# Moving one v chunk and the v tail ahead of the next batch's k and q halves, with a head pair's transposes exchanged to match

## The chip, the cores and the metric

One core of a Trainium2 chip runs the whole program. Times are device microseconds (us); the lower the better. A timed figure is the median of several executions. A profile is of one execution, with a trace of every engine. The span of an execution, from its first instruction to its last, is about 1.8 us shorter than its timed figure, so timed figures are compared with timed figures and spans with spans. A run counts as slow when it takes over 1.5% more than the fastest of the same kernel. The record also has the mean clock granted to TensorE in nearly every timed execution. Ratios are the mean time of one kernel's fast runs over the mean of the other's fast runs in the same rounds, so they are not quite the ratio of the medians that are quoted.

## The reference

Causal attention by blocks of 64 (8 batches, 8 heads, 576 positions, head size 64) is followed by a feed-forward layer with a gate, over 4608 tokens.

```
scores = (q @ k^T) / sqrt(64);  masked where block(i) < block(j), blocks of 64
attn   = softmax(scores) @ v                      # per batch and head
x      = attn as [4608, 512]
xn     = x / sqrt(mean(x*x) + 1e-6) * rms_g
out    = (silu(xn @ w_gate) * (xn @ w_val)) @ w_out
```

## The kernel before

The kernel is one long list of steps in a fixed order. Each engine executes its share strictly in that order, so a step that has to wait holds up everything behind it on its engine. Two strings matter here. INIT is the order of the first loads on GpSimd's queue, RAMP the order of the first compute steps.

```python
INIT = """
k1 q2 id k2 q1 k3 q3 v0 v1 v3 Ka Qa Kb Qb v2 vt W1 W0 W3 W2 qt O0 O1 VT V0 V2 V1 V3 h1 h0 h2 h7
h4 h3 h6 h5
"""
RAMP = """
... n0 Z n1 nr D11 D10 Z nx t3 Z a0 p D22 Z D12 D23 Z D20 a1 D21 D31 t0 D32 a2 D33 D30
nt t1 a3 t2 A0 U l l U U l U m0 U U m2 U B1 ...        # cut
"""
```

- `v0` to `v3`, `vt`: batch 0's v in four chunks of 128 positions, and its tail of 64 (two small transfers). `Ka Kb Qa Qb`: batch 1's k and q in halves of four heads. `W0` to `W3`: the gate and value weights in four blocks, two transfers each. `O0 O1`: the output weights WO in halves. `V..`: batch 1's v. `qt`, `h..`: tails and heads for batch 2.
- `t0` to `t3`: transposes on TensorE of batch 1's head pairs; t0 needs Ka and Qa, t3 needs Kb and Qb. They are first used much later, at `A0`.
- `a0`: the values of batch 0's first "late" head pair (query tiles 2 to 4). It needs every v chunk and the tail.
- `Dxy`: scores and exponentials of the late pairs. `nx`: a scaling on VectorE and ScalarE. `Z`: a dummy matmul that keeps TensorE's clock up. `U`: up projections of the feed-forward layer. `O`: one third of a down projection, four matmuls with WO. The other letters stay in their order and don't matter here.

```python
def values(self, part):                              # a0: every v chunk is read
    ...
    for j, t in enumerate(self.qts):
        for c in range(t + 1):
            mm(X[:, o:o + D + 1], self.PT[:, c0:c0 + P],
               VN[self.b % 2][:, c, 2 * self.hp + h, 0:D + 1], c == 0, c == t)

def load_down_weights(m0, m1):                       # O0: 0 to 6, O1: 6 to 12
    pool_dma(out=WO[:, m0:m1, :], in_=...)

def down(i, s, part):                                # O: four of twelve matmuls
    for m in range(part * 4, part * 4 + 4):
        mm(po, HT[:, m, s * P:(s + 1) * P], WO[:, m, :], m == 0, m == NMC - 1)
```

So the first down projection needs O1 at its seventh matmul. Transfers issued by GpSimd share eight semaphores in turn. In the order of instructions each of them waits, before it is issued, for the landing of the one eight places ahead.

The softmax here doesn't subtract the row's maximum and nothing guards it: scores larger than these inputs give would overflow.

## Time and profile before

| | before |
|---|---|
| timed, median (first runs; then with the runs beside the changed kernel) | 379.09; 379.18 us |
| span of the profiled run | 377.1 us |
| TensorE busy | 363.1 us (96%) |
| TensorE idle for the k and the q half at t3 | 1.30 + 1.08 us |
| granted clock from 20.15 to 24.40 us | 0.60 |
| first up projection | 32.23 us |
| first WO matmul | 45.35 us |

TensorE is nearly always busy, so a gain has to come from the few waits at the beginning. The rows are shown in the prediction. In a timeline row the first number is the start, the second the time, and a bracket at the end tells how long the engine had been idle and for whom.

### The profile page before, as it was taken

The page shows a single profiled execution, that of the slowest core. Times are in us where ns is not written, and L with a number is a line of the kernel's source. Part 1 is how long each engine was busy: PE and PEld are TensorE (multiplying, and loading weights), DVE is VectorE, ACT ScalarE, POOL GpSimd, SP SyncE. Part 2 cuts the span into 40 slices and gives each one's busy share as a digit, 9 for nine tenths or more (in the row PEclk, how much of TensorE's full clock was granted, in tenths as well). Part 3 has the DMA queues.
Part 4 walks back from the last instruction along what each step waited for, and adds up shares of the span by engine and source line. Part 5 has one row for each costly group of instructions (what it writes and reads, how often), then busy time and mean ns, then how long its engine had stood idle before and what let it go on. Part 6 is the DMA issues. An engine that isn't in the chain of part 4 may idle for free.

```text
span 377.1 us, 7796 instructions
## 1 busy us (share of the span) xinstructions
PE 363.1 (96%) x2953; PEld 188.3 (50%) x2993; DVE 248.9 (66%) x635; ACT 212.8 (56%) x368; POOL 138.7 (37%) x193
## 2 busy tenths in 40 slices
PE   8789999989999999999999999999999999999996
PEld 3458668645455445544454435544554444444442
DVE  6646867878875697648954894569668806724750
ACT  3967767865667657656683668267754313313321
POOL 8653697894887819446805000000000000000000
PEclk9989999999999999999999999999999999999999
DMA  9999999999999999998999427042101320011002
GB/s 161 183 202 200 183 142 158 154 168 142 167 133 185 181 92 137 178 138 84 133 152 95 95 49 141 30 98 42 51 30 28 92 83 29 2 55 56 2 20 92
DMA packets 158519, 41.12 MB, mean 109 GB/s; under 512 B 145169, under 2 KB 153873, under 8 KB 158482
## 3 DMA queue, kind: packets, MB, share of 16 engines
q0 software_dynamic: 103488, 18.59, 67.4%
q1 hardware_dynamic: 54258, 21.74, 28.9%
q8 instruction: 23, 0.38, 0.4%
q10 hardware_dynamic: 736, 0.30, 0.4%
q14 instruction: 14, 0.11, 0.1%
HBM read 37.75 MB, written 9.44 MB: 125 GB/s over the span
## 4 chain that ended last, share of the span: by engine, by line
PE 68%; DVE 14%; DMA 7%; issue 5%; ACT 3%; POOL 2%; DVEq 0%; ACTq 0%; POOLq 0%
PE f L122 63%; PE s L122 4%; DVE HT L116 4%; DVE th L116 3%; DVE XS L116 3%; DMA QKT<-QKN 3%; DMA HT<-in_q_dram 3%; POOL HT L102 1%; DMA XT<-XS 1%; ACT PT L116 1%; DVE XN L116 1%; DVE a L116 1%; ACT th L116 1%; ACT sq L116 1%; POOL VN L102 1%
## 5 line engine op out<-in xcount | busy, mean ns | idle before, releaser
L122 PE MATMUL f<-XT,WG 128*128 128x512 bf16 (+1 forms) x461 | 109.5, 357 | 2.2 <-DVE HT L116 0.6
L122 PE MATMUL f<-XT,WV 128*128 128x512 bf16 (+1 forms) x474 | 110.0, 357 | 1.0 <-DVE HT L116 0.6
L116 ACT ACTIVATE th<-f 128x512 f32<-128x512 f32 x108 | 64.6, 598 | 78.9 <-PE f L122 77.6
L116 ACT ACTIVATE PT<-s 128x1024 bf16<-128x1024 f32 (+2 forms) x100 | 95.6, 992 | 22.4 <-PE s L122 18.7
L116 DVE SCALAR_TENSOR_TENSOR th<-th,f 128x512 f32<-128x512 f32 x108 | 73.9, 684 | 48.1 <-ACT th L116 47.5
L122 PE MATMUL f<-WO,HT 128*128 128x512 bf16 x419 | 99.1, 379 | 1.0
L116 DVE TENSOR_TENSOR HT<-th,f 128x512 bf16<-128x512 f32 x108 | 74.1, 686 | 14.0 <-PE f L122 5.7
L122 PEld LDWEIGHTS <-WV 128*128 128x128 bf16 x480 | 46.8, 98 | 47.3 <-issue 1.3
L122 PEld LDWEIGHTS <-WG 128*128 128x128 bf16 x480 | 45.7, 98 | 45.4 <-issue 3.1
L122 PEld LDWEIGHTS <-HT 128*128 128x128 bf16 x432 | 40.7, 98 | 47.4 <-DVE HT L116 3.0
L102 POOL DMA_DIRECT2D QKN<-in_k_dram x60 | 47.0, 784 | 24.4 <-DMA QKT<-QKN 8.7
L102 POOL DMA_DIRECT2D QKN<-in_q_dram x60 | 47.0, 783 | 13.0 <-DMA VN<-in_v_dram 4.3
L116 ACT ACTIVATE ob<-f 128x512 f32<-128x512 f32 x36 | 21.5, 598 | 48.0 <-PE f L122 48.0
L102 POOL DMA_DIRECT2D VN<-in_v_dram x48 | 38.5, 861 | 19.6 <-PE f L122 17.1
L122 PE MATMUL f<-VN,PT 128*128 128x65 bf16 x960 | 37.8, 194 | 1.5 <-DVE XN L116 0.4
L122 PEld LDWEIGHTS <-PT 128*128 128x128 bf16 x960 | 34.5, 98 | 9.0 <-issue 2.2
L116 DVE TENSOR_TENSOR XN<-f,rd 128x320 f32<-128x320 f32 (+2 forms) x64 | 31.5, 491 | 2.2
L116 DVE MEMSET PT<- 64x64 uint32 (+1 forms) x116 | 11.4, 114 | 27.5 <-ACT PT L116 25.3
L116 DVE SCALAR_TENSOR_TENSOR XS<-XN,y,grow 128x512 bf16<-128x512 f32 x38 | 27.5, 748 | 0.4
L116 ACT ACTIVATE sq<-XN 128x512 bf16<-128x512 f32 x38 | 23.8, 627 | 2.0 <-DVE XN L116 1.7
L122 PE MATMUL s<-QKT 64*128 64x512 bf16 (+4 forms) x240 | 21.9, 294 | 0.0
L116 DVE RECIPROCAL rd<-f 128x5 f32<-128x5 f32 (+2 forms) x64 | 12.1, 190 | 13.0 <-PE f L122 11.6
(54 smaller groups left out, 132.3 us busy)
## 6 DMA issues: line engine op xcount, KB each, us to landing
out_dram<-ob SPq DMA_DIRECT2D x36, 256.0 KB, 2.3
VN<-in_v_dram POOLq DMA_DIRECT2D x32, 128.0 KB, 5.5
QKN<-in_k_dram POOLq DMA_DIRECT2D x48, 64.0 KB, 4.5
QKN<-in_q_dram POOLq DMA_DIRECT2D x48, 64.0 KB, 4.4
WG<-in_moe_w_gate_dram POOLq DMA_DIRECT2D x4, 384.0 KB, 10.4
WV<-in_moe_w_val_dram POOLq DMA_DIRECT2D x4, 384.0 KB, 11.0
WO<-in_moe_w_out_dram POOLq DMA_DIRECT2D x2, 768.0 KB, 11.2
XT<-XS SPq DMA_TRANSPOSE x39, 3.7
```

Source lines behind the costliest of these rows:

```text
L102: return chain("POOL", nc.gpsimd.dma_start(**kw))
L116: return lambda *a, **kw: chain(self.key, f(*a, **kw))
L122: pe(nc.tensor.matmul(dst, w, r, start=start, stop=stop))
```

## The change

The intent: TensorE stands waiting at t3 for Kb and Qb, and the work that follows, a0, needs v2 and the tail, which are queued behind them. Put those loads in front of the four halves, do a0 at once, do t0 (which needs only the first halves) after it, and t3 later in t0's old place.

```diff
-    k1 q2 id k2 q1 k3 q3 v0 v1 v3 Ka Qa Kb Qb v2 vt W1 W0 W3 W2 qt O0 O1 ...
+    k1 q2 id k2 q1 k3 q3 v0 v1 v3 v2 vt Ka Qa Kb Qb W1 W0 W3 W2 qt O0 O1 ...
...
-    e3 D02 Z Z n0 Z n1 nr D11 D10 Z nx t3 Z a0 p D22 Z D12 D23 Z D20 a1 D21 D31 t0 D32 a2 D33 D30
+    e3 D02 Z Z n0 Z n1 nr D11 D10 Z nx Z a0 t0 p D22 Z D12 D23 Z D20 a1 D21 D31 t3 D32 a2 D33 D30
```

(`...` marks cuts; nothing else changes.)

More of the change, by code (lines that the diff above doesn't have):

```diff
@@ L49 @@
     INIT = """
-    k1 q2 id k2 q1 k3 q3 v0 v1 v3 Ka Qa Kb Qb v2 vt W1 W0 W3 W2 qt O0 O1 VT V0 V2 V1 V3 h1 h0 h2 h7
+    k1 q2 id k2 q1 k3 q3 v0 v1 v3 v2 vt Ka Qa Kb Qb W1 W0 W3 W2 qt O0 O1 VT V0 V2 V1 V3 h1 h0 h2 h7
     h4 h3 h6 h5
```

## The prediction

> **What bounds the kernel now.** I read the page first, then the timeline of TensorE, ScalarE and GpSimd up to 62 us, the windows view, the list of DMA issues in narrow windows (for landing times), and the waits of TensorE over the rest of the run. First the page:
>
> ```profile
> PE 363.1 (96%) x2953; PEld 188.3 (50%) x2993; DVE 248.9 (66%) x635; ACT 212.8 (56%) x368; POOL 138.7 (37%) x193
> ...
> PEclk9989999999999999999999999999999999999999
> ```
>
> TensorE is busy for 363.1 of 377.1 us. From 60 us to the end its list of waits holds only 0.5 us (for an XT transpose), 0.4 us (XN) and about 1.2 us (HT). So what can be won lies in the first 30 us, and whatever is won there reaches the end only if no load that TensorE meets later was just in time. One slice, 18.9 to 28.3 us, also shows a clock of 8 tenths. The timeline of TensorE at that place (start, duration, engine, line, work, and in brackets the idle time before):
>
> ```profile
> 16.94 0.39 PE L122 MATMUL f<-zeros 128*128 128x512 bf16 x1
> 18.63 0.45 PE L248 MATMUL f<-ident,HT 96*64 96x96 bf16 x12 [1.30 <-DMA HT<-in_k_dram]
> 20.15 0.45 PE L248 MATMUL f<-ident,HT 96*64 96x96 bf16 x12 [1.08 <-DMA HT<-in_q_dram]
> 20.53 0.45 PE L122 MATMUL f<-zeros 128*128 128x512 bf16 x1
> 20.78 1.52 PE L122 MATMUL f<-VN,PT 128*128 128x65 bf16 x24
> ...
> 24.65 0.90 PE L122 MATMUL f<-VN,PT 128*128 128x65 bf16 x24
> ```
>
> The step t3 (transposes of batch 1's last head pair) stands second in the program order after 17.3 us and needs the last k half and the last q half. TensorE waits 1.30 + 1.08 = 2.38 us for them. Then a0 (the values of the first late pair) takes 1.52 us where the same work four microseconds later takes 0.90: the clock has dropped. The windows view (us; then busy time of PE, PEld, DVE, ACT, POOL with counts; clock; DMA share; GB/s) says the same:
>
> ```profile
> 17.30:20.15 2.85, 0.48 (x13) 0.31 (x12) 2.47 (x13) 2.06 (x3) 1.48 (x2) 1.00 1.78 180
> 20.15:24.40 4.25, 4.25 (x51) 2.50 (x53) 1.10 (x3) 1.97 (x4) 3.58 (x5) 0.60 1.33 204
> 24.40:30.00 5.60, 5.19 (x126) 4.07 (x125) 3.06 (x8) 5.33 (x11) 1.83 (x3) 1.00 1.31 202
> ```
>
> TensorE is idle first, then at 0.60 of its clock; from 24.4 on ScalarE is the bound (5.33 of 5.60 us busy with the exponentials). The issues of single transfers (size, us to landing), first Qb (issued 10.18), then v2 (10.84):
>
> ```profile
> HT<-in_q_dram POOLq DMA_DIRECT2D x1, 288.0 KB, 9.9
> ...
> VN<-in_v_dram POOLq DMA_DIRECT2D x1, 128.0 KB, 10.0
> ```
>
> Qb lands at 10.18 + 9.9 = 20.08, v2 at 20.84. In the same way Ka lands at 8.17 + 8.0 = 16.2, Qa at 8.85 + 8.3 = 17.2, Kb at 9.51 + 9.1 = 18.6, the two v tails at 11.72 + 9.3 = 21.0 and 12.34 + 8.9 = 21.2. So a0, which needs v2 and the tails, stands at a second gate right behind the first: moving t3 away alone would win nothing.
>
> **What the Trainium skill says.** (1) "DMA: Bandwidth & Descriptors", section "Two DMAs through the same engine are not ordered": within one queue descriptors start in order, and only the semaphore says that data has landed. The trace agrees: the six landings above come in queue order, 16.2 to 21.2. The order in the queue is therefore what the change can move. (2) The same page, "Specifications": line rate needs transfers of at least 512 B. The trace agrees in direction: from 10 to 11 us, all packets under 512 B, 154 GB/s; from 14 to 15 us, larger ones, 206 GB/s. A v chunk is thus dearer than its size suggests. (3) "TensorE: Matmul & The Clock Gate", "Part 1: The HAM clock gate": the clock falls to half after about one idle window of 3.4 us. Here 2.38 us of idle with one 0.45 us burst in between was enough: 0.50 in the narrow windows from 20.8 to 22.5 us. (4) "Perfetto Trace Analysis", "DMA Instruction — SWDGE (GPSIMD)": the profiled end of such an issue is the end of writing descriptors, not of moving data. It agrees: 0.73 us for the issue of Qb, 9.9 us to landing.
>
> **The change part by part.** No instruction is added or removed; the orders of instructions show that SP is the same, and on GpSimd v2 and the two tails (3 transfers) pass in front of four halves.
>
> *Loads.* The three cost what they cost now behind Qb: 21.24 - 20.08, about 1.2 us. v3 landed by 12.94 (the issue of the first weight block, which waits for it, did not wait). So v2 and the tails land near 12.9 + 1.2 = 14.1, and the four halves 1.2 us later each: Ka 17.4, Qa 18.4, Kb 19.8, Qb 21.3. Everything behind (weights, WO, batch 1's v) has the same bytes in front of it and lands when it did.
>
> *TensorE.* After its warm-up matmuls, near 17.6, a0 finds its data and takes 0.9 at full clock: 18.5. t0 finds Ka and Qa: 19.2. D22 starts then instead of at 22.24, 3 us earlier. t3 now stands after D31, near 23.5, when Qb has long landed.
>
> *ScalarE.* It can't follow by 3 us: its in-order list has the XS scaling (19.33, set by VectorE's root chain, which nothing moves), then the copy of t0's q (0.65), then D22's exponential, near 20.5 instead of 22.85. From there to 30.2 it is nearly solid, with the same work (t3's copy for t0's). So the first up projection moves from 32.23 by about 2.3 us, to near 29.9.
>
> *What meets the earlier TensorE.* This row of TensorE's timeline is the first use of WO:
>
> ```profile
> 45.35 5.35 PE L122 MATMUL f<-WO,HT 128*128 128x512 bf16 x23
> ```
>
> The order of instructions puts a wait for the second half of WO at the seventh of these 24 matmuls: 45.35 + 6 x 0.216 = 46.65. That half was issued at 33.14 and landed 12.1 us later, at 45.24. Slack: 1.4 us. The other gates have more: WG and WV of block W2 land at 21.86 + 12.9 = 34.8 and 22.59 + 14.2 = 36.8 for uses at 37.48 and 39.13 (2.7 and 2.3 us); batch 1's last v chunk lands near 49.2 for a use at 51.2 (2.0); the transpose for batch 2's second pair, issued at 58.44, lands 8.2 us later, at 66.6, for 69.06 (2.4). So of 2.3 us, 0.9 turn into a wait for WO, and 1.4 pass. Later gates would let 1.4 through, and from there on TensorE is back to back. Sum: 2.38 idle and some 1.5 of slow clock removed locally (3.9), 2.3 after ScalarE, 1.4 after WO: 379.09 - 1.4 = 377.7, put at 377.8 because VectorE and the DMA rings will give back a little.
>
> **Rivals.** *All of the 2.3 us arrive* (376.8): if WO lands earlier than now. Against: the queue has the same bytes and never runs dry, the rings moving about 200 GB/s throughout. *Nothing arrives* (379.1): if a later gate with no slack takes it, for instance the XT transposes at 82 us, for which TensorE already waits 0.5, or batch 1's v, had I read its landing 2 us too early. For it: the DMA share is in the nines up to 226 us, and these loads stand at absolute times. Against: XT hangs on VectorE's work, which moves along with TensorE. *Worse* (379.5 to 380): the halves, 1.2 us later, are waited for at t0, or the idle time moves to 20 to 24 us and the clock drops there instead. Against: t0 needs only the first halves, and Ka and Qa are due before 18.5; even a drop would hide behind ScalarE.
>
> **Range and chances.** The WO gate caps the win at 1.4, and a small wait at another gate can cut it to nothing; the three runs before spread over 0.6 us. I take 377.1 to 378.9. Two per cent would be 7.6 us, more than twice all idle time and slow clock in this stretch: faster 0.005, same 0.985, slower 0.01.
>
> **What would show it.** In the profile after: no wait for HT at t3; a0 near 17.6 and taking 0.9 us; a clock of 1.00 between 20 and 24.4; D22's exponential near 20.5; the first up projection near 29.9; a new wait of about 0.9 us for WO just after 44.3; and from 52 us on every TensorE instruction 1.4 us earlier than before, to the end. If the new wait is not at WO but elsewhere, or the lead is gone by 85 us, the step on slack is wrong. If the first up projection moves by 3 us or more, the step on ScalarE is wrong.

## The result

The changed kernel took 376.86 us (median of 4 runs, 376.60 to 377.62), the kernel before 379.18 us beside it. The ratio is 0.9942, 95% interval 0.9923 to 0.9961: a gain of 0.6%, inside the 2% called "same". The time lies 0.24 us below the range of 377.1 to 378.9 that was forecast.

The page of the changed kernel:

```profile
PE 360.6 (96%) x2953; PEld 187.5 (50%) x2993; DVE 248.6 (66%) x635; ACT 212.3 (57%) x368; POOL 138.8 (37%) x193
...
PEclk9999999999999999999999999999999999999999
```

TensorE is busy 2.5 us less with the same 2953 matmuls: the slice at a lower clock is gone. Its timeline:

```profile
17.07 0.61 PE L122 MATMUL f<-zeros 128*128 128x512 bf16 x2
17.51 0.89 PE L122 MATMUL f<-VN,PT 128*128 128x65 bf16 x24
18.33 0.70 PE L248 MATMUL f<-ident,HT 96*64 96x96 bf16 x24
...
20.70 0.38 PE L122 MATMUL f<-zeros 128*128 128x512 bf16 x1 [0.65 <-DVE XN L116]
...
29.37 1.05 PE L122 MATMUL f<-XT,WG 128*128 128x256 bf16 x8
...
36.61 1.05 PE L122 MATMUL f<-XT,WV 128*128 128x256 bf16 x8 [0.27 <-DMA WV<-in_moe_w_val_dram]
...
42.83 1.47 PE L122 MATMUL f<-WO,HT 128*128 128x512 bf16 x5
44.92 4.05 PE L122 MATMUL f<-WO,HT 128*128 128x512 bf16 x18 [0.63 <-DMA WO<-in_moe_w_out_dram]
```

a0 starts at 17.51 with no wait, at full clock, and t0 follows at once. The first up projection comes at 29.37 instead of 32.23, 2.86 us earlier. Before the matmuls at 36.61 TensorE waits 0.27 us for the value weights of block W2, which landed at 36.56; after that the lead is 39.13 - 36.61 = 2.52 us, and at the first WO matmul still 45.35 - 42.83 = 2.52. Then, in the first down projection, TensorE stands 0.63 us for the second half of WO and goes on at 44.92. Before, the seventh matmul was due at 45.35 + 6 x 0.216 = 46.65, so 1.73 us of the lead pass. The windows view of the same three stretches as in the prediction (us; busy PE, PEld, DVE, ACT, POOL; clock; DMA share; GB/s):

```profile
17.30:20.15 2.85, 2.75 (x61) 1.96 (x60) 2.43 (x14) 2.16 (x4) 2.31 (x4) 1.00 1.31 202
20.15:24.40 4.25, 3.41 (x72) 2.31 (x72) 2.60 (x5) 4.10 (x9) 1.46 (x3) 1.00 1.31 203
24.40:30.00 5.60, 5.00 (x121) 4.14 (x118) 3.51 (x9) 4.52 (x9) 1.84 (x3) 1.00 1.32 204
```

The idle stretch and the half clock are gone, and ScalarE is busy 4.10 of 4.25 us where it was busy 1.97. On ScalarE, D22's exponential and the copy of the first feed-forward input show how the lead grows. Two rows from the timeline of before, then two from that of the changed kernel:

```profile
22.85 0.70 ACT L116 ACTIVATE PT<-s 128x640 bf16<-128x640 f32 x1 [1.57 <-PE s L122]
...
29.36 0.83 ACT L116 ACTIVATE XT<-f,gscale 128x256 bf16<-128x256 bf16 x2
```

```profile
20.61 1.30 ACT L116 ACTIVATE PT<-s 128x640 bf16<-128x640 f32 x2
...
26.50 0.83 ACT L116 ACTIVATE XT<-f,gscale 128x256 bf16<-128x256 bf16 x2
```

The lead is 22.85 - 20.61 = 2.24 us at the first and 29.36 - 26.50 = 2.86 at the second, with the same work between.

From 50 us on TensorE's lead can be read off the first scores of batch 2 (61.43 before, 59.69 after: 1.74 us), those at 253.73 (252.01: 1.72 us), and those at 267.04 (265.01: 2.03 us). The spans differ by the same 2.03 us (377.09 and 375.06).

### The profile page after: what moved, and what is told of

Same layout as the page of the kernel before. It is cut to its first block, busy times and chain, and to the rows that moved or that the text cites. A ratio compares the mean times of both kernels' runs of the same rounds, so it can differ in the third digit from the quotient of the medians.

```text
span 375.1 us, 7794 instructions
## 1 busy us (share of the span) xinstructions
PE 360.6 (96%) x2953; PEld 187.5 (50%) x2993; DVE 248.6 (66%) x635; ACT 212.3 (57%) x368; POOL 138.8 (37%) x193
## 3 DMA queue, kind: packets, MB, share of 16 engines
q0 software_dynamic: 103488, 18.59, 66.5%
## 4 chain that ended last, share of the span: by engine, by line
PE 66%; DVE 13%; DMA 10%; issue 5%; ACT 3%; POOL 3%; DVEq 0%; POOLq 0%; ACTq 0%
PE f L122 62%; DMA WV<-in_moe_w_val_dram 4%; DVE HT L116 4%; DVE XS L116 3%; PE s L122 3%; DMA WO<-in_moe_w_out_dram 3%; DVE th L116 3%; DMA VN<-in_v_dram 2%; DMA XT<-XS 1%; ACT PT L116 1%; POOL HT L102 1%; DVE XN L116 1%; ACT th L116 1%; ACT sq L116 1%; POOL VN L102 1%
## 5 line engine op out<-in xcount | busy, mean ns | idle before, releaser
L122 PEld LDWEIGHTS <-QKT 64*128 64x128 bf16 (+1 forms) x264 | 10.3, 94 | 18.8 <-issue 15.1
```

What stands on the lines that cost most here:

```text
L122: pe(nc.tensor.matmul(dst, w, r, start=start, stop=stop))
```

## The experiments

The starting theory was the prediction's, corrected by the result. **Theory**: the change opens two gates in a row (halves, then v2 and the tails), the lead is passed on by ScalarE and by the clock, and WO's landing cuts it. **Rivals**: one gate only; a clock effect that is hidden behind ScalarE; a cap elsewhere; chance. "Landing" below is the last of a transfer's sixteen part-landings that the trace records. All twelve runs gave correct results; each was timed in five rounds. They ran in three calls of four, and the kernels of one call shared one chip and the runs of the kernel before.

### c1: the kernel before again

No edit. Expected:

> Control: the kernel before, unchanged, for a second trace. Ratio 1.000 within 0.002. Two theories of why the second half of WO landed at 44.9 us in the changed kernel and at 45.3 us before. Theory (order of the queue): it is systematic, because behind v3 one of the sixteen part-landings of each k and q half stays 1.5 us or more behind the other fifteen in this order; then it lands here at 45.2 to 45.4 again and the first k half lands near 16.2 with that straggler. Rival (jitter of one ring from run to run): it lands anywhere between 44.8 and 45.4.

Measured: ratio 1.0001 (0.9979 to 1.0024). WO's second half landed at 45.69 us. Of the first k half fifteen parts had landed by 14.88 and the last at 15.67, against 14.19 and 16.16 in the first trace. Both lie outside what the theory expected, and WO's landing outside the rival's range too. A late part is there again, but how late it is varies.

### c2: the changed kernel again

No edit. Expected:

> The changed kernel again, for a second trace and a closer time. Theory: the wait for the second half of WO is there again, 0.5 to 0.8 us; TensorE leads the kernel before by 1.6 to 1.9 us from 50 us on; ratio 0.9945 to 0.9955 (1.7 to 2.1 us). If the 2.3 us between the medians is real and not spread, the ratio is 0.994 or below and the trace shows a further lead won after 100 us.

Measured: 376.50 against 378.17 us, ratio 0.9960 (0.9938 to 0.9982). The first up projection came at 29.33 us. The wait for WO was there again:

```profile
44.67 4.05 PE L122 MATMUL f<-WO,HT 128*128 128x512 bf16 x18 [0.56 <-DMA WO<-in_moe_w_out_dram]
```

WO landed at 44.63. The lead at batch 2's first scores is 61.19 - 59.44 = 1.75 us against c1. The ratio is a little above the expected range. In the traces the lead then grew to 100.44 - 97.96 = 2.48 us, and the spans differ by 2.81 us, because the wait for the XT transposes near 80 us (see e6) was 0.93 us in c1 and 0.24 in c2. The gap between the medians was 1.67 us here and 2.32 in the first runs.

### e1: WO in front of qt

```diff
- ... Qb W1 W0 W3 W2 qt O0 O1 VT V0 V2 V1 V3 ...
+ ... Qb W1 W0 W3 W2 O0 O1 qt VT V0 V2 V1 V3 ...
```

> Changed kernel with the two halves of WO loaded in front of the four small qt transfers instead of behind them. Theory (WO caps the win): the second half lands about 1 us earlier, near 43.9; the 0.63 us wait at the seventh WO matmul goes to 0.1 or less; the lead at 50 us grows by 0.5 to 0.7 us and lasts to the end: ratio to the kernel before 0.9925 to 0.9937. Rival (another gate stands right behind, batch 1's v or the QKT transposes of batch 2): the wait moves there and the ratio stays at that of the changed kernel, 0.9945 to 0.9955.

Measured: 378.60 us, ratio 1.0012 (0.9989 to 1.0036): the whole gain was lost. WO landed at 43.60, 1.0 us earlier than in c2, and was not waited for. But TensorE then waited for batch 1's v:

```profile
49.33 0.37 PE L122 MATMUL f<-VN,PT 128*128 128x65 bf16 x7 [0.57 <-DMA VN<-in_v_dram]
50.37 0.80 PE L122 MATMUL f<-VN,PT 128*128 128x65 bf16 x21 [0.67 <-DMA VN<-in_v_dram]
```

GpSimd's timeline says why. The columns are the same:

```profile
40.08 0.89 POOL L102 DMA_DIRECT2D VN<-in_v_dram  x1 [3.20 <-DMA WO<-in_moe_w_out_dram]
44.60 2.63 POOL L102 DMA_DIRECT2D VN<-in_v_dram  x3 [3.63 <-issue]
```

Three of the four v chunks now stand behind WO's second half in such a way that the transfer eight places ahead is that half or comes after it, so they are issued only at 44.60, after it has landed (at 43.60; the further 1.0 us is not explained). It isn't the bytes: the same loads stand in front of batch 1's v in c2, and from 45.83 to 47.50 us no part of a load of GpSimd's queue landed here. The rival was right about the place, but it expected the changed kernel's ratio: the gate behind WO was moved onto the path by this very edit. Not all of the loss is accounted for. This trace, of the fastest of the six runs, still leads c1 by 61.19 - 60.31 = 0.88 us at batch 2's first scores.

### e2: the kernel before with its clock kept up

```diff
- nr D11 D10 Z nx t3 Z a0
+ nr D11 D10 Z nx Z Z Z Z Z Z t3 Z a0
```

> Kernel before with six more dummy matmuls in front of t3, which fill the 1.3 us in which TensorE waits for the k half, so that its clock is not lowered; loads and order as before. It separates the clock from the wait. Theory (the slow clock reaches ScalarE, which starves on late scores): clock 1.00 from 20.1 to 24.4 us, the first up projection at 31.5 to 31.8 instead of 32.2, nothing takes it back, ratio 0.9982 to 0.9988 (0.5 to 0.7 us). Rival (my prediction: the slow clock is hidden behind ScalarE): the up projection stays within 0.1 us of 32.2, ratio 1.000.

Measured: 377.13 against 378.17 us, ratio 0.9977 (0.9948 to 1.0006; the interval just includes 1). The trace is clear. In the windows view the clock stays at 1.00, and the up projection comes at 31.18, which is 0.81 us earlier than in c1 (31.99) and 1.05 earlier than in the first trace, more than the 0.4 to 0.7 that were expected:

```profile
20.15:24.40 4.25, 4.09 (x79) 2.81 (x79) 1.33 (x3) 2.69 (x5) 3.58 (x5) 1.00 1.33 203
```

With the waits at t3 still there (0.3 and 1.0 us), the slow clock alone was worth 0.8 to 1.0 us at that place. It was not hidden behind ScalarE. ScalarE is busy 2.69 us in this stretch, 1.97 before: it had been waiting for late scores.

### e3: the order of the loads alone

```diff
- ... v0 v1 v3 Ka Qa Kb Qb v2 vt W1 ...        # RAMP stays as before
+ ... v0 v1 v3 v2 vt Ka Qa Kb Qb W1 ...
```

> Only the order of the loads is changed; t3 stays in front. Theory (two gates in a row, both have to go): t3 waits as before, for halves that now land behind v2 and the tails; from the landings in the two traces of the changed kernel (last k half 18.6 to 19.2, last q half 20.1 to 20.7) a0 starts between 20.7 and 21.3 us, no earlier than before, and the clock is lowered again; first up projection 31.9 to 32.8 us; ratio 1.000 to 1.002. By the working of my prediction (halves 1.2 us later each) a0 would start near 22.0 and the ratio would be 1.003. Rival (the loads are what matters): the up projection well below 31.5 us.

Measured: 379.28 against 379.03 us, ratio 1.0021 (0.9989 to 1.0053). The first up projection came at 32.75. TensorE's timeline:

```profile
19.16 0.45 PE L248 MATMUL f<-ident,HT 96*64 96x96 bf16 x12 [1.74 <-DMA HT<-in_k_dram]
20.67 0.45 PE L248 MATMUL f<-ident,HT 96*64 96x96 bf16 x12 [1.06 <-DMA HT<-in_q_dram]
```

t3 waits for the halves, which land 0.5 us later than before, not 1.2. Nothing is gained.

### e4: the order on TensorE alone

```diff
- nx t3 Z a0 p D22 ... D21 D31 t0 D32          # INIT stays as before
+ nx Z a0 t0 p D22 ... D21 D31 t3 D32
```

> Only the order on TensorE is changed; the loads stay as before. Theory (two gates): the wait for the halves goes, but a0 waits at its third matmul for v2, which lands at 20.7 to 20.9 us, so it still ends near 22.2, on a lowered clock; first up projection 31.9 to 33.0 us; ratio 0.999 to 1.002. Rival (one gate, the halves): a0 near 17.6 us, up projection near 29.5, ratio near 0.995.

Measured: ratio 1.0035 (1.0005 to 1.0066), 380.24 against 379.03 us. TensorE now waits for v2:

```profile
20.18 0.82 PE L122 MATMUL f<-VN,PT 128*128 128x65 bf16 x22 [2.50 <-DMA VN<-in_v_dram]
```

This is the second gate by itself. The first up projection came at 32.10, the span was 376.9 us. The ratio is above the expected range. The traced run is the fastest of the six (378.70 us); the median is 1.5 us above it, and the other five runs had a mean clock of 0.985 to 0.991 where the traced one had 0.995. Parts alone win nothing; together they win.

### e5: the second half of WO in two transfers

```diff
-  "O1": lambda: load_down_weights(NMC // 2, NMC)}
+  "O1": lambda: load_down_weights(NMC // 2, 3 * NMC // 4),
+  "O2": lambda: load_down_weights(3 * NMC // 4, NMC)}
- ... qt O0 O1 VT ...
+ ... qt O0 O1 O2 VT ...
```

> Changed kernel with the second half of WO loaded in two transfers of half the size, same place in the queue. Theory (TensorE waits at the seventh WO matmul for bytes that only the tenth and later need): the first part lands near 43.0 and is not waited for; the second lands near 44.8, and the tenth matmul waits 0.2 us or less; lead at 50 us 2.1 to 2.3 us instead of 1.75; ratio to the kernel before 0.9930 to 0.9950. Rival: the extra transfer shifts the window of eight and delays batch 1's v, a wait of 0.4 us or more appears at VN near 49 us and the lead is 1.75 or less.

Measured: 376.33 against 379.03 us, ratio 0.9940 (0.9911 to 0.9969). The two parts landed at 42.65 and 44.58, and no wait for WO appeared. But in this trace the clock fell to half from 22.2 to 25.6 us, so the first up projection came only at 30.55 and TensorE reached WO at 43.67, when hardly anything was left to wait for (lead at batch 2's first scores 1.68 us, 2.1 to 2.3 expected). The trace doesn't test the split. It shows that the changed kernel can lose a clock window as well.

### e6: v in front of qt, weight blocks in order of use

```diff
- ... W1 W0 W3 W2 qt O0 O1 VT V0 V2 V1 V3 h1 h0 h2 h7 h4 h3 h6 h5
+ ... W0 W1 W2 W3 O0 O1 VT V0 V2 V1 V3 qt h1 h0 h2 h3 h4 h7 h6 h5
```

> Changed kernel with weight blocks in order of use, WO and batch 1's v in front of qt, and batch 2's second head pair loaded earlier. In the run with WO in front of qt, three of the v loads were issued only once WO had landed, because a transfer waits for the one eight places ahead; here they wait for weight blocks instead. Theory (that window and not the bytes made the wait for v): WO's second half lands near 43.6 with no wait, the last v chunk by 48.2, no wait for VN at 48 to 50 us, lead at 50 us 2.4 to 2.9 us; if the transposes for batch 2 keep up, ratio 0.9920 to 0.9940. Rival: the later qt delays these transposes and TensorE waits 0.5 us or more at QKT between 58 and 70 us.

Measured: 376.87 us, ratio 0.9955 (0.9926 to 0.9985). WO landed at 44.21, no wait for it, none for v. The first WO matmul starts at 43.11 and TensorE runs through all of them:

```profile
43.11 5.35 PE L122 MATMUL f<-WO,HT 128*128 128x512 bf16 x23
```

The first up projection came at 29.99, so the lead there was 32.23 - 29.99 = 2.24 us, and at batch 2's first scores it is 61.43 - 59.20 = 2.23: all of it passes, where the changed kernel loses 2.86 - 1.74 = 1.12 us. So the weights, WO above all, were the cap. That WO and v come earlier here without e1's wait fits e1's reading, that the waiting of issues made its loss. The ratio is no better than the changed kernel's and missed the expected 0.9920 to 0.9940. The lead then meets the next gate:

```profile
80.22 1.02 PE L122 MATMUL f<-XT,WG 128*128 128x512 bf16 x3 [1.23 <-DMA XT<-XS]
```

Behind it the lead is 100.28 - 98.49 = 1.79 us. This wait was 0.52, 0.93 and 0.88 in the three traces of the kernel before and 0.80, 0.24 and 0.99 in those of the changed kernel. So the comparison of single traces is uncertain by a few tenths here. The QKT wait that the rival named did not come.

### c3: the changed kernel, third time

> The changed kernel for the third time, beside the two variants of it on one chip. Second half of WO at 44.6 to 45.0 us again (order of the queue), where jitter alone would put it at up to 45.7, as in the runs with the old order. If no clock window falls to half, first up projection near 29.4 and lead at 61 us 1.7; ratio 0.994 to 0.996.

Measured: 377.56 against 378.81 us, ratio 0.9967 (0.9945 to 0.9990). This trace lost a clock window too, from 22.36 to 25.77 us:

```profile
20.15:24.40 4.25, 3.13 (x43) 2.02 (x43) 2.16 (x6) 3.47 (x7) 2.10 (x3) 0.76 1.32 204
```

Its first up projection came at 30.96, 1.6 us after that of the first trace, and it had no wait for WO (which landed at 45.13). The guess that the new order always lands WO by 45.0 missed.

### e7: the changed kernel with its idle stretch filled

```diff
- p D22 Z D12 D23 Z D20
+ p D22 Z D12 Z Z Z D23 D20
```

> Changed kernel; the dummy matmul that waits for VectorE to empty its bank is replaced by three that write a free bank, ahead of D23, so that the idle time at 20 to 21 us is filled. One of five traces with the changed kernel's order of both parts had a window at half clock there and started the first up projection 1.2 us later. Theory: that window never comes; two of eleven timed runs of the changed kernel stood 1.1 us above the others, and these vanish; median equal to that of the changed kernel within 0.3 us, smaller spread, ratio 0.9935 to 0.9955. Rival: the clock window is not what sets the slow runs; the spread stays the same.

Measured: 376.90 us, ratio 0.9953 (0.9930 to 0.9976), clock 1.00. The first up projection came at 29.31, and the wait for WO was 0.80 us. The six timed runs lie between 376.59 and 378.20, so the spread did not shrink; all six had a mean clock of 0.998 or more. On that chip its median is 0.66 us under that of c3, which the intervals don't separate.

### e8: the same, with WO's second half in two transfers

> The same with the second half of WO in two transfers. With the clock kept up TensorE now arrives at the seventh WO matmul near 44.1, before the old second half lands. Theory: no wait there, the tenth matmul waits 0.2 us or less; lead at 61 us 2.0 to 2.4 us where the changed kernel has 1.7; but the XT transposes near 80 us, for which TensorE waits 0.2 to 1.2 us in all traces, take some of it back: lead at 98 us 1.7 to 2.2, ratio 0.9930 to 0.9950. Rival (the win passes whole): lead at 98 us as at 61 us.

(The edits are those of e5 and e7 together.) Measured: 376.47 us, ratio 0.9943 (0.9917 to 0.9970), 1.1 us under c3; the intervals overlap. Its trace was spoilt by two windows at half clock much earlier (12.6 to 19.4 us), so a0 started only at 20.70 and there was no wait for WO to test. The theory about the tenth matmul stays untested. With e5 (0.9940) it has the lowest ratio of the variants, but neither is shown to beat the changed kernel.

### c4: the kernel before, third time

> The kernel before once more, as a control on the same chip. Ratio 1.000 within 0.002; one window of 3.4 us at half clock beginning between 20.5 and 22 us; second half of WO at 45.0 to 45.7 us.

Measured: 379.02 us, ratio 1.0002 (0.9977 to 1.0028). One window at half clock from 20.98 us, WO at 45.09. All as expected.

## Why the prediction was right or wrong

**Right: where the gain starts.** Both waits at t3 vanished, a0 started at 17.51 (17.6 forecast) and took 0.89 (0.9), D22's exponential came at 20.61 (20.5). That two gates stood in a row was right as well: e3 and e4 each open one and win nothing.

**Right in kind, wrong in size: the landings.** The halves were put 1.2 us later each. In the changed trace they landed at 16.29, 17.71, 19.17 and 20.71 where they had landed at 16.16, 17.16, 18.59 and 20.11: 0.1 to 0.6 later. The step took the landing times as one stream. (The passage cited under (1) speaks of one queue of one DMA engine; the prediction left that out.) The part-landings show that fifteen of sixteen parts of the first k half were in by 14.19 and only the last at 16.16. In the changed trace the fifteenth came at 15.61, 1.4 us later where 1.2 was forecast, but the last at 16.29. So the landing says how late the slowest part is, and for this half that slack took up nearly all of the delay. v2 and the tails landed at 14.92 to 15.32, not near 14.1, still in time for a0.

**Wrong: "even a drop would hide behind ScalarE", and the 2.3 us at the first up projection.** It was 2.86. ScalarE is the bound only from 24.4 us on. In the slow stretch it waited for scores, and e2 puts the slow clock at 0.8 to 1.0 us there. With the larger lead the last block of weights was late too: its slack was put at 2.3 us, and 2.86 - 2.52 = 0.34 us of the lead ended there.

**The step that set the number: "the same bytes in front of it and lands when it did", and "the WO gate caps the win at 1.4".** This is the step that failed, in size and not in kind. That there is a cap at WO, and that most of the rest of the lead ends there, was right: the wait of 0.63 us stands at the seventh matmul, which took 2.52 - 1.73 = 0.79 us of the lead, and e6, which takes the gate away, carries 2.23 us where the changed kernel carries 1.74. The slack was mis-sized. WO landed at 44.88, not 45.24, and so 1.73 us passed instead of 1.4. Over the traces, the old load order landed it at 45.28, 45.69, 45.09 (kernel before), 45.60 (e2) and 45.08 (e4), and the new one at 44.88, 44.63, 45.13 (changed kernel), 44.95 (e3) and 44.75 (e7). The means are 45.35 and 44.87, the ranges touch, and within one call the gap runs from 0.1 us (e3 and e4) to 1.1 (c1 and c2). So the order of the queue may move this landing by some 0.5 us, but part of the 0.40 us in the first pair can be luck; why the last part is slow is open.

**A term that the sum didn't have: 0.31 us near 251 us.** In the kernel before, VectorE starts one product late. Row of before, then of the changed kernel:

```profile
251.42 0.69 DVE L116 TENSOR_TENSOR HT<-th,f 128x512 bf16<-128x512 f32 x1 [0.47 <-PE f L122]
```

```profile
249.34 0.69 DVE L116 TENSOR_TENSOR HT<-th,f 128x512 bf16<-128x512 f32 x1
```

With TensorE's lead of 1.72 us taken off, the first is 0.36 us late, although TensorE's own work stands the same. From the scores near 253 to those near 267 us all five traces with the old order of steps take 13.29 to 13.32 us, all nine with the new order 12.99 or 13.00. It belongs to the order of steps and not to the loads (e3 has the old value, e4 the new one). The cause isn't known. Beside the exchange, the traces of the two orders differ by one semaphore wait on VectorE and one on ScalarE, which the old order has more. So the late product is the 576th VectorE instruction of the trace in the old order and the 575th in the new one. In all fourteen traces only two VectorE instructions start more than 0.15 us after their engine was free and their last wait had ended: the 576th in the five old ones, and the 64th in ten. Both are multiples of 64. That points to the fetching of instructions and not to the data, but no run tests it.

**The sum** for the first pair of traces is then 1.73 + 0.31 = 2.04 us, against a difference of 2.03 between the spans and 1.4 in the forecast. What the forecast feared as give-back didn't come on balance (1.74 us of lead at 61 us, 1.72 at 253), so the 0.1 us kept back for it went the wrong way as well. The timed gaps of medians were 2.32, 1.67 and 1.25 us (4, 6 and 6 runs of the changed kernel), weighted by runs 1.7. So the first runs lie at the favourable end of what this kernel does.

**How much of the timed gain is the clock.** Two of the six traces of the changed kernel or its variants without extra dummies lost a clock window (c3, e5). In the timed runs the mean clock shows it: one window of 3.41 us at half clock takes 0.0045 off it. Of 45 runs of the kernel before, 7 had a mean clock of 0.998 or more and took 377.5 us on average, 28 had 0.993 to 0.995 and took 378.5, and 10 had 0.991 or less and took 379.7. Of the 16 runs of the changed kernel 12 had 0.998 or more and took 377.1, and 4 had 0.993 to 0.995 and took 377.2. So at full clock the two kernels are only some 0.4 us apart, which so few runs don't separate from nothing, and the larger part of the timed gain goes with clock windows that the changed kernel loses less often. The runs fell into these groups by themselves, so this is not an experiment. But e2 points the same way: the clock alone gave 1.04 us between the medians (with an interval that just includes nothing) where c2 had 1.67. The prediction had counted the slow clock as hidden, so its sum had no term for this.

**The rivals of the prediction.** "Nothing arrives" and "worse" are out. "All of the 2.3 us arrive" came near the first timed number, but by luck: of the 2.86 us the last weights took 0.34 and WO 0.79, and the 0.31 us near 251 us came on top. Two small slips had no effect: the landings listed are seven, not six, and 7.6 us is about twice the 3.9 us of that stretch, not more.

## What to carry to other kernels

A step that waits for a load is often followed by another that waits for the next load in the same queue: change the order of the loads and of the steps together, because either alone can win nothing. Before counting on a lead, list the later loads with the times at which they land and are needed, and expect the lead to be cut to the smallest slack; before moving a load forward, look at which transfers will have to wait for its landing to be issued. And count a lowered TensorE clock by what waits for its results, not by whether another engine looks busy afterwards.

## What the Trainium skill lacked or had wrong

- "TensorE: Matmul & The Clock Gate", section "Part 1: The HAM clock gate": its table says that the clock falls after an idle window of about 3.4 us. Here the half clock did last 3.41 us, or twice that (e8), but it also followed windows in which TensorE had been busy for 2.29 (c3) and 2.28 (e5) of 3.41 us, and not ones with 2.40 (e1), 2.48 (first trace of the changed kernel) and 2.77 us (c2). In e2, with dummy matmuls of 512 columns, it did not follow one with 2.15 us. So no wholly idle window is needed, and busy time alone doesn't decide. (Further down, in "A second HAM failure mode: psum-queue depth-cycling", the same page has a kernel whose clock goes up and down through short idle times, without a figure for them.) (The windows are counted in steps of 3.41 us from the trace's own clock records.)
- "DMA: Bandwidth & Descriptors", section "Latency and other measured facts": it says that two of the sixteen DMA engines are usually slower and gives no size. Here the last of the sixteen part-landings of one k half came 2.0 us after the fifteenth (16.16 and 14.19 us) in one run and 0.8 us (15.67 and 14.88) in another of the same kernel. The trace doesn't tell which engine it was.
- I found no page with the stall that hangs on the order of steps far from where it was changed: 0.31 us near 251 us, in five of five traces with the old order and in none of nine with the new one.
